# Wider weight conversions, one reciprocal per visit, and a plan that knows the PSUM banks, in a sparse attention and feed-forward kernel

## The chip, the core and the metric

The kernel runs on one core of one Trainium2 chip. The metric is the device time of one execution in microseconds (us). Three runs of the kernel before took 1224.89, 1225.10 and 1226.91 us; the median is 1225.1 us.

## What is computed

q, k and v hold 8 batches of 8 heads with 576 rows of 64 values. For each head, scores are q times k transposed, divided by 8; scores more than tau below the largest of their row are dropped; the rest go through a softmax and weight v. The heads are laid side by side to 4608 rows of 512 values, and each row x goes through a feed-forward layer.

```
scores = scale * np.matmul(q, k.transpose(0, 1, 3, 2))
thresh = np.max(scores, axis=-1, keepdims=True) - tau
scores = np.where(scores >= thresh, scores, -1000000000.0)
attn = softmax(scores); attn_out = np.matmul(attn, v)      # cut
h = x @ w_in;  r = np.maximum(h, 0.0);  g = s * (r * r) + b
out = g @ w_out
```

The weights w_in and w_out (512 x 2048 and 2048 x 512) arrive as 64-bit floats and are turned into 32-bit ones on the core.

## The kernel before, in words

**Attention.** A *visit* is one pair of heads of one batch over one half of the rows: 64 visits of four *tiles* each (two heads, two blocks of 128 rows), and in every second visit a fifth tile with the last 64 rows of both heads (288 tiles). TensorE (PE) writes a tile's 128 x 576 scores into a PSUM tile. VectorE (DVE) takes the row limit (L416, in place) and adds tau (L421); ScalarE (ACT) takes the exponential into an SBUF tile em or tr (L427); DVE reads the scores again to drop what is below the limit and sums the rest (L430), then takes the reciprocal (L433). From visit 4 on GpSimd (POOL) scales the tile by it (L435); in visits 0 to 3 (*unscaled*) the shares are put in later (L498, L520, L521). In the first 8 visits PE transposes each tile: a small block of 64 columns (L445) and four blocks of 128 (L447), which ACT copies out (L454 and L456). Later visits transpose on DVE and by DMA. After a visit's last tile PE multiplies with v (L507) into the bank pv.

**PSUM.** Five tiles hold the eight banks: s0, s1 and o have two each, pv and h one each. In visits 0 to 3 scores go round s0, s1 and o; the small transposes go back into the score tile that was just read (its first columns), the large ones into h or pv.

**Feed-forward.** After four visits a block of 256 rows is split into a high and a low part (L621 on ACT, L623 on DVE, two halves), and 16 steps f follow: 12 matmuls into h (L637), square of the positive part on ACT (L644, L645), high part (L647), low part on POOL (L648), and 6 matmuls into o (L654), three per half of the rows. L674 takes o out. 18 blocks make 288 steps.

**Weights.** For each f, 512 KB of w_in and 512 KB of w_out are loaded (L546, L549). Each half is converted by itself: ACT L582, DVE L585 (a shift) and L587 (shift and or), ACT L591, POOL L593; DVE L596 adds w_out up. The first 16 steps need one conversion each.

**The order.** Every operation is recorded with its engine, costs and the keys that it reads and writes. `Plan.run` (L62 to L88) lists them in 144 ways (18 settings by 8 rounds), plays each through a model of the engines, and keeps the best; the engines then run exactly that order. The plan before knows keys, not banks: an operation that has to wait because another engine is in the same bank is not seen by it, while the recording layer adds that wait.

Of the kernel before, what the change touches and what calls it, by code (L numbers as in the profile page):

```python
# [29 lines left out]
SCALED_LATE = 4  # L30


class Plan:
# [6 lines left out]
    SLOW = (1, 1.2), (2, 1.3), (3, 1.5), (4, 1.3)  # L40
# [6 lines left out]
    def add(self, engine, cost, emit, r=(), w=(), at=0.0, port=False, tiled=False):  # L47
# [12 lines left out]
        self.ops.append((engine, cost[0], cost[-1], emit, deps, at, port or engine == "POOL", tiled))  # L60

    def run(self):  # L62
# [7 lines left out]
        for share, later, stretch in [(a, b, c) for a in self.SHARES for b in self.LATER for c in self.STRETCH]:  # L70
            rank, early = [o[5] for o in ops], set()
            for _ in range(ROUNDS):
# [6 lines left out]
                if best is None or worth < best[0]:  # L79
                    best = worth, order  # L80
# [6 lines left out]
        self.order = best[1]  # L87
        return [ops[n][3] for _, n in self.order]  # L88

# [3 lines left out]
    def played(self, order, seed, cold, hand=60, to_pe=150, same=40):  # L93
        ops, free, done, port, mode = self.ops, {}, [0.0] * len(self.ops), 0.0, False
        late = random.Random(seed)
        for _, n in order:
            e, busy, ready, _, deps, _, shared, tiled = ops[n]
# [4 lines left out]
            for d in deps:  # L102
                if ops[d][0] != e:
                    t = max(t, done[d] + (to_pe if e == "PE" else hand))
                elif e != "PE":
                    t = max(t, done[d] + same)
            if shared and port > t:
                t = port
# [10 lines left out]
            done[n] = t + busy + tail  # L119
        return max(done) / 1000  # L120

    def ordered(self, before, after, rank, busy, done, back):
# [10 lines left out]
        order, port, mode = [], 0.0, False  # L133
        for _ in ops:
# [17 lines left out]
            if e == "PE" and mode and not ops[n][7]:  # L152
                for at, m in sorted(there[e]):
                    if ops[m][7] and at < rank[n] + self.NEAR:
# [4 lines left out]
                        break  # L159
            if e == "PE":  # L160
                t += self.TURN * (mode != ops[n][7])
                mode = ops[n][7]
            if ops[n][6] and port > t + self.PASS:
                for at, m in sorted(there[e]):
                    if not ops[m][6] and busy[m] < port - t + self.OVER:
                        there[e].remove((at, m))
                        heapq.heapify(there[e])
                        heapq.heappush(there[e], (rank[n], n))
                        n = m
                        break  # L170
            if ops[n][6]:
                t = max(t, port)
                port = t + busy[n]
            order.append((t, n))
# [17 lines left out]
def tile_attention_ffn(ctx: ExitStack, tc: tile.TileContext, qT, kT, v, tau, w_in, w_out, s, b, out):  # L192
    nc = tc.nc
    P = 128
# [29 lines left out]
    st = [const(f"st{i}", [P, 8]) for i in range(12)]  # L224
# [59 lines left out]
    class Visit:  # L284
# [10 lines left out]
        def scores_in(self, i, j):  # L295
            return f"s{i % 2}" if self.split else f"s{j}" if self.late else ("s0", "s1", "o")[i % 3]
# [59 lines left out]
    def scores(vs, i, t):  # L356
        n = vs.n
        if t is None:
# [4 lines left out]
            pe(970, both, [("k", n)] + vs.kd, ["s0"], i - SCORES_AHEAD)  # L363
# [13 lines left out]
    def split_scores(vs, i, j, t):  # L377
# [8 lines left out]
        pe(531, products, [(x, j) for x in ("z", "qh", "ql")], [sk], i - SCORES_AHEAD)  # L386
# [22 lines left out]
    def tile_of(vs, i, j, t):  # L409
        sk = vs.scores_in(i, j)  # L410
        ps, ks_, st8 = flat[sk], f"st{i % 12}", st[i % 12]
# [6 lines left out]
            scalar1=nsc, scalar2=None, op0=ALU.mult, op1=ALU.min, accum_out=st8[:, 0:1]),  # L418
            [sk, "nsc"], [sk, (ks_, 0)], i - 0.6)
        if vs.pe:  # L420
            dve((127, 208), lambda: nc.vector.tensor_scalar(  # L421
                out=st8[:, 1:2], in0=st8[:, 0:1], scalar1=tau8, scalar2=None, op0=ALU.add),
                [(ks_, 0), "nsc"], [(ks_, 1)], i - 0.4)
        else:
            act((186, 285), lambda: nc.scalar.activation(out=st8[:, 1:2], in_=st8[:, 0:1], func=AF.Identity, bias=tau8),  # L425
                [(ks_, 0), "nsc"], [(ks_, 1)], i - 0.4)
        act((632, 740), lambda: nc.scalar.activation(  # L427
            out=ev, in_=ps[:, S0:S0 + S], func=AF.Exp, bias=st8[:, 0:1], scale=-1.0),
            [sk, (ks_, 0)], [em_k], i - 0.5)
        dve((742, 830), lambda: nc.vector.scalar_tensor_tensor(  # L430
            out=eb, in0=ps[:, S0:S0 + S + 1], scalar=st8[:, 1:2], in1=eb, op0=ALU.is_le, op1=ALU.mult,
            accum_out=st8[:, 2:3]), [sk, em_k, (ks_, 1)], [em_k, (ks_, 2)], i)
        dve((90, 165), lambda: nc.vector.reciprocal(out=st8[:, 4:5], in_=st8[:, 2:3]), [(ks_, 2)], [(ks_, 4)], i)  # L433
        if not vs.unscaled:
            pool((795, 825), lambda: nc.gpsimd.tensor_scalar(  # L435
                out=ev, in0=ev, scalar1=st8[:, 4:5], scalar2=zero, op0=ALU.mult, op1=ALU.add), [em_k, (ks_, 4)], [em_k], i)

        if vs.pe:
            tt, kt = ps[0:T, 0:P], (sk, "t")
            kp = ["pv"] if vs.late or i % 2 else ["h0", "h1"]  # L440
            tp = bank[kp[0].strip("01")]
            tp = tp.rearrange("p (c q) -> p c q", c=NQ)

            def transposes():
                nc.tensor.transpose(out=tt, in_=ev[:, M:S], identity=ident)  # L445
                for c in range(NQ):
                    nc.tensor.transpose(out=tp[:, c], in_=ev[:, c * P:(c + 1) * P], identity=ident)  # L447
            pe(575, transposes, [em_k, "ident"], [kt] + kp, i + 0.5)
            parts = [(j, 4 * t, 0, P)] if t is not None else [(h, NB // 32, h * T, h * T + T) for h in range(2)]
            for h, n0, c0, c1 in parts:  # L450
                nn = (c1 - c0) // 32
                e = er[:, vs.n, h, n0:n0 + nn].rearrange("p n (c q) -> p c n q", c=5)
                ke = [("er", vs.n, h, n0 + n) for n in range(nn)]
                act((46 + 28 * nn, 146 + 28 * nn), lambda e=e, c0=c0, c1=c1, nn=nn: nc.scalar.copy(  # L454
                    out=e[0:T, NQ], in_=tt[:, c0:c1].rearrange("p (n q) -> p n q", n=nn)), [kt], ke, i + 0.5)
                act((68 + 100 * nn, 176 + 100 * nn), lambda e=e, c0=c0, c1=c1, nn=nn: nc.scalar.copy(  # L456
                    out=e[:, 0:NQ], in_=tp[:, :, c0:c1].rearrange("p c (n q) -> p c n q", n=nn)), kp + ke, ke, i + 0.5)
# [407 lines left out]
```

## Time and profile before

| | |
|---|---|
| median of three runs | 1225.1 us |
| the profiled execution | 1225.36 us, its span 1223.5 us |
| PE busy | 1194.7 us (98%) |
| DVE, ACT, POOL busy | 802.5, 766.9, 700.8 us |
| mean granted TensorE clock | 0.993 |

Busy time is the share in which an engine had something in flight. The rows below were read from the views of this execution: waits (who waited for whom, total, times, longest), windows (busy time of each engine in a stretch of the span), groups of like instructions, and the timeline (start, duration, engine, line, tile; in brackets the idle time ahead of it and what ended it). One instruction's duration is longer than the distance to the next on the same engine; where a price of an instruction in a stream is meant, it is that distance.

### The profile page before, as it was taken

To read this page: it belongs to the slowest core of one execution; us is meant where nothing else is said; L and a number is where in the kernel's file an instruction comes from. 1 tells how busy PE (TensorE), PEld (TensorE's weight loads), DVE (VectorE), ACT (ScalarE), POOL (GpSimd) and SP (SyncE) were. 2 spreads that over 40 slices of the span, in tenths; PEclk is the share of its full clock that TensorE was granted. 3 is DMA by queue.
4 is the path that set the end of the run, shared out by engine and by line. 5 is a ranking of instruction groups with operands and counts; after the bars stand their busy time and mean duration, and the time that the engine had idled before them with its cause. 6 is when DMAs were issued, how large, how long until landed. Compare 5 with 4: busy or idle time off the path is not lost.

```text
span 1223.5 us, 24575 instructions
## 1 busy us (share of the span) xinstructions
PE 1194.7 (98%) x7958; PEld 987.4 (81%) x7958; DVE 802.5 (66%) x2162; ACT 766.9 (63%) x1890; POOL 700.8 (57%) x806
## 2 busy tenths in 40 slices
PE   7789999999999999999999999999999999999998
PEld 5467778888887888878887888888888888878987
DVE  7997876777776776756666667666666576663021
ACT  5777756666665765666666666566656665654443
POOL 1466845766665775656675666667656675652200
PEclk8999999999999999999999999999999999999999
DMA  8661256677767766666566756556756666652000
GB/s 301 210 206 43 64 137 157 155 184 184 179 153 173 185 169 162 155 157 169 138 172 166 172 142 157 142 151 159 193 137 158 156 159 152 170 134 69 4 18 18
DMA packets 259536, 180.69 MB, mean 148 GB/s; under 512 B 83536, under 2 KB 238160, under 8 KB 259408
## 3 DMA queue, kind: packets, MB, share of 16 engines
q1 hardware_dynamic: 259120, 178.98, 57.5%
q8 instruction: 64, 1.05, 0.4%
q14 instruction: 64, 0.52, 0.1%
q10 hardware_dynamic: 288, 0.13, 0.0%
HBM read 87.03 MB, written 9.44 MB: 79 GB/s over the span
## 4 chain that ended last, share of the span: by engine, by line
PE 94%; DVE 3%; ACT 1%; issue 1%; DMA 0%; ACTq 0%; DVEq 0%
PE h L637 34%; PE o L654 33%; PE pv L507 13%; PE s L384 9%; PE s L373 2%; PE s L395 1%; DVE s L416 1%; DVE k L587 1%; PE pv L447 1%; DVE tr L430 0%; DMA qr<-in_q_dram 0%; DVE em L430 0%; PE s L445 0%; ACT em L427 0%; ACT er L456 0%
## 5 line engine op out<-in xcount | busy, mean ns | idle before, releaser
L637 PE MATMUL h<-xh,w 128*128 128x256 f32 x2304 | 467.0, 284 | 1.2 <-ACT g L644 1.2
L637 PEld LDWEIGHTS h<-xh,w 128*128 128x128 f32 x2304 | 377.5, 190 | 28.1 <-issue 7.6
L654 PE MATMUL o<-w,gh 128*128 128x512 f32 x1152 | 364.9, 398 | 0.6 <-DVE em L674 0.6
L416 DVE TENSOR_SCALAR_CACHE_REDUCE s<-s,nsc 128x576 f32<-128x576 f32 x283 | 230.4, 820 | 153.8 <-PE s L384 119.5
L648 POOL TENSOR_TENSOR gl<-g,gh 128x256 fp32r<-128x256 f32 x272 | 204.6, 753 | 212.7 <-ACT gh L647 187.1
L637 PE MATMUL h<-xl,w 128*128 128x256 f32 x1152 | 325.1, 282 | 0.0
L435 POOL TENSOR_SCALAR em<-em,st,zero 128x576 f32<-128x576 f32 x262 | 220.0, 841 | 139.2 <-DVE st L433 94.1
L430 DVE SCALAR_TENSOR_TENSOR em<-s,st,em 128x577 f32<-128x577 f32 x268 | 217.0, 811 | 83.9 <-ACT st L425 54.1
L427 ACT ACTIVATE em<-s,st 128x576 f32<-128x576 f32 x268 | 197.7, 738 | 66.9 <-DVE s L416 41.0
L654 PEld LDWEIGHTS o<-w,gh 128*128 128x128 f32 x1152 | 196.5, 189 | 35.1 <-issue 11.3
L654 PE MATMUL o<-w,gl 128*128 128x512 f32 x576 | 224.5, 390 | 0.0
L644 ACT ACTIVATE g<-h 128x256 f32<-128x256 f32 x288 | 110.4, 383 | 181.2 <-PE h L637 165.4
L637 PEld LDWEIGHTS h<-xl,w 128*128 128x128 f32 x1152 | 219.0, 190 | 5.5
L468 DVE STREAM_TRANSPOSE tr<-em 128x512 f32<-128x512 f32 x252 | 178.1, 707 | 52.0 <-POOL em L435 45.4
L507 PE MATMUL pv<-er,vb 128*64 128x256 f32 (+1 forms) x1280 | 170.3, 411 | 0.0
L349 POOL TENSOR_TENSOR k<-kr,k 64x576 fp32r<-64x576 f32 x104 | 149.0, 1434 | 37.1 <-ACT k L348 26.9
L647 ACT CAST gh<-g 128x256 fp32r<-128x256 f32 x288 | 116.2, 404 | 43.2 <-PE o L654 40.2
L384 PE MATMUL s<-k 128*128 128x288 f32 x832 | 142.4, 296 | 0.0
L507 PEld LDWEIGHTS pv<-er,vb 128*64 128x64 f32 x1280 | 85.7, 136 | 66.8 <-issue 11.8
L384 PEld LDWEIGHTS s<-k 128*128 128x128 f32 x832 | 127.2, 188 | 15.3 <-issue 2.4
L654 PEld LDWEIGHTS o<-w,gl 128*128 128x128 f32 x576 | 108.2, 188 | 24.6
L645 ACT ACTIVATE g<-g 128x256 f32<-128x256 f32 x288 | 120.0, 417 | 4.8
(108 smaller groups left out, 939.5 us busy)
## 6 DMA issues: line engine op xcount, KB each, us to landing
er<-tr SPq DMA_DIRECT2D x448, 160.0 KB, 3.2
kr<-in_k_dram SPq DMA_DIRECT2D x116, 288.0 KB, 4.1
vb<-in_v_dram SPq DMA_DIRECT2D x128, 128.0 KB, 3.0
qr<-in_q_dram SPq DMA_DIRECT2D x56, 160.0 KB, 4.3
er<-tr SPq DMA_DIRECT2D x112, 80.0 KB, 2.3
w<-in_moe_w_in_dram SPq DMA_DIRECT2D x16, 512.0 KB, 6.3
w<-in_moe_w_out_dram SPq DMA_DIRECT2D x16, 512.0 KB, 5.4
out_dram<-oo SPq DMA_DIRECT2D x30, 256.0 KB, 2.3
```

Source lines behind the costliest of these rows:

```text
L349: pool((1500, 1500), lambda: nc.gpsimd.tensor_tensor(out=z()[D:P], in0=kr[D:P, j], in1=z()[D:P].bitcast(F32), op=ALU.subtract), rk + [("z" ...
L384: nc.tensor.matmul(flat[sk][:, S0 + hf * HS:S0 + (hf + 1) * HS], lazy["q"][:, x, j, qc], lazy["k"][:, j, cs], start=(x == 0), stop=(x == 1))
L416: dve((740, 875), lambda: nc.vector.tensor_scalar(out=ps[:, S0:S0 + S], in0=ps[:, S0:S0 + S], scalar1=nsc, scalar2=None, op0=ALU.mult, op1 ...
L427: act((632, 740), lambda: nc.scalar.activation(out=ev, in_=ps[:, S0:S0 + S], func=AF.Exp, bias=st8[:, 0:1], scale=-1.0), [sk, (ks_, 0)], [ ...
L430: dve((742, 830), lambda: nc.vector.scalar_tensor_tensor(out=eb, in0=ps[:, S0:S0 + S + 1], scalar=st8[:, 1:2], in1=eb, op0=ALU.is_le, op1= ...
L435: pool((795, 825), lambda: nc.gpsimd.tensor_scalar(out=ev, in0=ev, scalar1=st8[:, 4:5], scalar2=zero, op0=ALU.mult, op1=ALU.add), [em_k, ( ...
L468: nc.vector.transpose(out=to[:, :, 0:NQ].rearrange("p m c q -> p m (c q)"), in_=ev[:, 0:M].rearrange("p (m r) -> p m r", m=4))
L507: nc.tensor.matmul(ps[j * D:(j + 1) * D, 0:32 * nb], vb[r, n, j, c], er[r, n, j, 0:nb, 32 * c:32 * c + 32], start=(c == 0), stop=(c == 4))
L637: nc.tensor.matmul(ps, w[:, c, :], x[:, c, :], start=(c == 0 and i == 0), stop=(c == NC - 1 and i == 2))
L645: act((322, 417), lambda: nc.scalar.activation(out=g, in_=g, func=AF.Square), [f"g{k}"], [f"g{k}"], at)
L648: do((712, 740), lambda: eng.tensor_tensor(out=lo, in0=g, in1=hi.bitcast(F32), op=ALU.subtract), [f"g{k}", f"gh{n}"], [f"gl{n}"], at)
L654: nc.tensor.matmul(bank["o"][:, t, :], a[:, ts_], w, start=(f == 0 and i == 0), stop=(f == NF - 1 and i == 2))
```

## The change

1. **Conversions 1024 wide.** Both halves of a weight step are converted together: one L655 on ACT for two L582, one L658 and one L660 on DVE for two L585 and two L587, one L663 for two L591. The two POOL operations stay. The wide operations wait until both halves have landed.
2. **One reciprocal for an unscaled visit.** Its four row sums stand side by side, and L490 runs once, after the fourth tile (4 for 16).
3. **Banks.** Unscaled visits use s0 and s1 alone for scores. Transposes leave the score tiles: in visits 0 to 3 they go to o, pv and h, from visit 4 on both kinds go to pv, the small one (L511) after the large one (L508) was copied out.
4. **The plan.** It keeps the last use of each bank and waits for it in listing and playing (`banks`, `free_at`, `used`), the prices of a few PE operations and the slow-down factors of the model are other numbers, and 28 numbers name random shifts of ranks (`shifted`) that are laid over the best order, after which the order is listed again.

```diff
+SHIFTS = (75, 80, 103, 117, 141, 184, 274, 284, 571, 923, 1025, 1061, 1146, 1562, 1708, 1768, 1775, 1850, 1896, 2348, 2463, 2483, 2540, 2693, 2702, 2859, 3035, 3099)
-    SLOW = (1, 1.2), (2, 1.3), (3, 1.5), (4, 1.3)
+    SLOW = (1, 1.0), (2, 1.1), (3, 1.3), (4, 1.1)
+    def free_at(self, n, t, last, tail, hand):
+        for b, writes in self.ops[n][8]:
+            for e, wrote, at, rest in last.get(b, ()):
+                if e != self.ops[n][0] and (writes or wrote):
+                    t = max(t, at + (rest if tail is None else tail) + hand)
+        return t
+        for n in SHIFTS:
+            rank = self.shifted(n, order, rank)
+            order = self.ordered(before, after, rank, busy, done, False)
-    st = [const(f"st{i}", [P, 8]) for i in range(12)]
+    st = [const(f"st{i}", [P, 4, 5]) for i in range(6)]
-            return f"s{i % 2}" if self.split else f"s{j}" if self.late else ("s0", "s1", "o")[i % 3]
+            return f"s{i % 2}" if self.split else f"s{j}"
-        dve((90, 165), lambda: nc.vector.reciprocal(out=st8[:, 4:5], in_=st8[:, 2:3]), [(ks_, 2)], [(ks_, 4)], i)
+        if not vs.unscaled or k_ == 3:
+            k0 = 0 if vs.unscaled else k_
+            dve((90, 165), lambda: nc.vector.reciprocal(out=sv[:, 3, k0:k_ + 1], in_=sv[:, 2, k0:k_ + 1]),
...
-            tt, kt = ps[0:T, 0:P], (sk, "t")
-            kp = ["pv"] if vs.late or i % 2 else ["h0", "h1"]
+            if vs.late:
+                tp, kp = bank["pv"], ["pv"]
+                tt, kt = tp[0:T, 0:P], kp
+            elif i % 2:
+                tt, kt, tp, kp = bank["pv"][0:T, 0:P], ["pv"], bank["o"][:, 0], ["o0"]
+            else:
+                tt, kt, tp, kp = bank["o"][0:T, 1, 0:P], ["o1"], bank["h"], ["h0", "h1"]
...
-        for u, k in (0, "i"), (1, "o"):
-            act((565, 680), lambda u=u: nc.scalar.activation(
-            dve2((340, 420), lambda u=u: nc.vector.tensor_scalar(
-            dve2((602, 686), lambda u=u: nc.vector.scalar_tensor_tensor(
+        act((1100, 1210), lambda: nc.scalar.activation(
+        dve2((607, 690), lambda: nc.vector.tensor_scalar(
+        dve2((1140, 1220), lambda: nc.vector.scalar_tensor_tensor(
...
```

The DVE at the start, before: the first two pairs of tiles (s_104 and s_105 are s0 and s1), with narrow conversions between them.

```order
L416 TENSOR_SCALAR s_104,st_71<-s_104,nsc 128x576
L416 TENSOR_SCALAR s_105,st_72<-s_105,nsc 128x576
L421 TENSOR_SCALAR st_71<-st_71,tau_67 128x1
L421 TENSOR_SCALAR st_72<-st_72,tau_67 128x1
L430 SCALAR_TENSOR_TENSOR em_83,st_71<-s_104,st_71,em_83 128x577
L585 TENSOR_SCALAR xh<-xh 128x512
L433 RECIPROCAL st_71<-st_71 128x1
L430 SCALAR_TENSOR_TENSOR em_84,st_72<-s_105,st_72,em_84 128x577
L587 SCALAR_TENSOR_TENSOR xh<-w_128,xh 128x512
L433 RECIPROCAL st_72<-st_72 128x1
L416 TENSOR_SCALAR o,st_73<-o,nsc 128x576
L416 TENSOR_SCALAR s_104,st_74<-s_104,nsc 128x576
```

The same place now (s_98 and s_99 are s0 and s1):

```order
L471 TENSOR_SCALAR s_98,st_71<-s_98,nsc 128x576
L471 TENSOR_SCALAR s_99,st_71<-s_99,nsc 128x576
L479 TENSOR_SCALAR st_71<-st_71,tau_67 128x1 x2
L485 SCALAR_TENSOR_TENSOR em_77,st_71<-s_98,st_71,em_77 128x577
L485 SCALAR_TENSOR_TENSOR em_78,st_71<-s_99,st_71,em_78 128x577
L471 TENSOR_SCALAR s_98,st_71<-s_98,nsc 128x576
L471 TENSOR_SCALAR s_99,st_71<-s_99,nsc 128x576
L479 TENSOR_SCALAR st_71<-st_71,tau_67 128x1 x2
```

The second pair now uses the tiles that the first one has just left, and no conversion stands between them. Later pairs have wide conversions between them, as here between the pairs of visit 2 (DVE now):

```order
L485 SCALAR_TENSOR_TENSOR em_78,st_73<-s_99,st_73,em_78 128x577
L660 SCALAR_TENSOR_TENSOR k<-w_195,k 128x1024
L595 TENSOR_TENSOR x_85<-pv,x_85 128x256
L668 TENSOR_TENSOR bias_t<-bias_t,k 128x512
L658 TENSOR_SCALAR k<-k 128x1024
L471 TENSOR_SCALAR s_98,st_73<-s_98,nsc 128x576
```

Every pair from the third on has one to five such operations between its end and the next pair's scores. PE at the first feed-forward step, before (tile 16 and 17 are em_83 and em_84):

```order
L362 MATMUL s_104<-kr,k 128x288 x2
L445 MATMUL s_104<-k,em_83 64x128
L447 MATMUL pv<-k,em_83 128x128 x4
L445 MATMUL s_105<-k,em_84 64x128
L447 MATMUL pv<-k,em_84 128x128 x4
L637 MATMUL h<-xh,w_280 128x256
L637 MATMUL h<-xl,w_280 128x256
```

And now (em_77, em_78 and tr_79 are tiles 16 to 18):

```order
L508 MATMUL pv<-k,em_77 128x128 x4
L511 MATMUL pv<-k,em_77 64x128
L709 MATMUL h<-xh,w_252 128x256
L709 MATMUL h<-xl,w_252 128x256
L709 MATMUL h<-xh,w_252 128x256 x2
L709 MATMUL h<-xl,w_252 128x256
L709 MATMUL h<-xh,w_252 128x256
L415 MATMUL s_98<-kr,k 128x288 x2
L508 MATMUL pv<-k,em_78 128x128 x4
L511 MATMUL pv<-k,em_78 64x128
L508 MATMUL pv<-k,tr_79 128x128 x4
L709 MATMUL h<-xh,w_252 128x256
```

The first half of the step (six matmuls) now stands ahead of the fifth tile's scores and of tile 17's transposes, the second half behind tile 18's.

## Rows read from the trace of the kernel before

**Rows 1.** The page: busy time (share, instructions) and 40 slices of the span.
```profile
PE 1194.7 (98%) x7958; PEld 987.4 (81%) x7958; DVE 802.5 (66%) x2162; ACT 766.9 (63%) x1890; POOL 700.8 (57%) x806
PE   7789999999999999999999999999999999999998
```
**Rows 2.** Windows: start:end length, busy (instructions) of each engine, PEclk, DMA.
```profile
10.00:40.00 30.00, 23.29 (x141) 14.62 (x141) 28.51 (x81) 22.52 (x47) 7.96 (x6) 0.87 0.83 286
40.00:70.00 30.00, 21.65 (x131) 13.30 (x131) 28.51 (x80) 20.70 (x43) 12.33 (x10) 0.89 0.66 211
78.00:150.00 72.00, 69.96 (x463) 52.63 (x463) 58.89 (x142) 55.48 (x141) 51.95 (x52) 1.00 0.22 67
150.00:1130.00 980.00, 980.00 (x6608) 818.48 (x6607) 665.19 (x1808) 621.71 (x1550) 609.45 (x705) 1.00 0.64 158
```
**Rows 3.** Waits of PE, 72 to 150 us.
```profile
PE s L445 <- ACT tr L427: 1.5, 1, 1.5
PE s L445 <- DVE tr L430: 1.3, 1, 1.3
PE pv L447 <- ACT er L456: 0.6, 1, 0.6
PE h L637 <- ACT g L644: 0.2, 1, 0.2
```
**Rows 4.** Timeline of DVE from its first tile on.
```profile
8.57 0.82 DVE L416 TENSOR_SCALAR_CACHE_REDUCE s<-s,nsc 128x576 f32<-128x576 f32 x1 [2.66 <-PE s L373]
9.32 0.82 DVE L416 TENSOR_SCALAR_CACHE_REDUCE s<-s,nsc 128x576 f32<-128x576 f32 x1
10.06 0.39 DVE L421 TENSOR_SCALAR st<-st,tau 128x1 f32<-128x1 f32 x2
10.41 0.82 DVE L430 SCALAR_TENSOR_TENSOR em<-s,st,em 128x577 f32<-128x577 f32 x1
11.15 0.42 DVE L585 TENSOR_SCALAR xh<-xh 128x512 int32<-128x512 int32 x1
11.49 0.16 DVE L433 RECIPROCAL st<-st 128x1 f32<-128x1 f32 x1
12.29 0.69 DVE L587 SCALAR_TENSOR_TENSOR xh<-w,xh 128x512 int32<-128x512 int32 x1
12.89 0.15 DVE L433 RECIPROCAL st<-st 128x1 f32<-128x1 f32 x1
```
**Rows 5.** Timeline of DVE and PE around the first staging and the first step.
```profile
69.47 0.68 DVE L623 TENSOR_TENSOR xl<-x,xh 128x512 fp32r<-128x512 f32 x1
70.84 0.36 PE L637 MATMUL h<-xh,w 128*128 128x256 f32 x1
72.23 0.28 PE L637 MATMUL h<-xh,w 128*128 128x256 f32 x1
```
**Rows 6.** Groups of DVE by shape, 8.5 to 69.5 us: busy, mean ns.
```profile
L587 DVE SCALAR_TENSOR_TENSOR k<-w,k 128x512 int32<-128x512 int32 x11 | 10.0, 906 | 0.0
L585 DVE TENSOR_SCALAR k<-k 128x512 int32<-128x512 int32 x12 | 5.7, 483 | 0.0
```
**Rows 7.** Timeline of PE: scores of a pair, at either clock.
```profile
60.66 1.97 PE L373 MATMUL s<-kr,qr 64*128 64x288 f32 x8
72.44 1.24 PE L373 MATMUL s<-kr,qr 64*128 64x288 f32 x8
```
**Rows 8.** Timeline of PE: from L654 into L507, and into L654.
```profile
83.01 0.39 PE L654 MATMUL o<-w,gl 128*128 128x512 f32 x1
83.33 3.06 PE L507 MATMUL pv<-er,vb 128*64 128x320 f32 x20
90.37 0.39 PE L654 MATMUL o<-w,gl 128*128 128x512 f32 x1
90.60 0.62 PE L654 MATMUL o<-w,gh 128*128 128x512 f32 x2
```
**Rows 9.** Timeline of DVE and PE at the end of the span.
```profile
1214.58 0.43 DVE L648 TENSOR_TENSOR gl<-g,gh 128x256 fp32r<-128x256 f32 x1 [2.40 <-ACT gh L647]
1218.25 0.74 PE L654 MATMUL o<-w,gh 128*128 128x512 f32 x2 [0.58 <-DVE em L674]
1219.26 1.27 DVE L674 SCALAR_TENSOR_TENSOR em<-o,s_t,bias_t 128x256 f32<-128x256 f32 x3 [1.07 <-PE o L654]
```

More of the change, by code (lines that the diff above doesn't have):

```diff
@@ L94, in played @@
         ops, free, done, port, mode = self.ops, {}, [0.0] * len(self.ops), 0.0, False
-        late = random.Random(seed)
+        late, last = random.Random(seed), {}
         for _, n in order:
-            e, busy, ready, _, deps, _, shared, tiled = ops[n]
+            e, busy, ready, _, deps, _, shared, tiled, _ = ops[n]
             t = free.get(e, 0.0)
@@ L106, in played @@
                     t = max(t, done[d] + same)
+            if ops[n][8]:
+                t = self.free_at(n, t, last, None, to_pe if e == "PE" else hand)
             if shared and port > t:
@@ L119, in played @@
             done[n] = t + busy + tail
+            if ops[n][8]:
+                self.used(n, t + busy, tail, last)
         return max(done) / 1000
@@ L132, in ordered, with delay @@
                 heapq.heappush(coming[o[0]], (0.0, n))
-        order, port, mode = [], 0.0, False
+        order, port, mode, last = [], 0.0, False, {}
+        def delay(n, t):
+            at = max(t, port) if ops[n][6] else t
+            if not ops[n][8]:
+                return at - t
+            hand = self.TO_PE if ops[n][0] == "PE" else self.HANDOVER
+            return self.free_at(n, at, last, done[n] - busy[n] if back else None, hand) - t
         for _ in ops:
@@ L159, in ordered @@
                         break
+            wait = delay(n, t)
+            if wait > self.PASS:
+                for at, m in sorted(there[e]):
+                    if delay(m, t) <= self.PASS and busy[m] < wait + self.OVER:
+                        there[e].remove((at, m))
+                        heapq.heapify(there[e])
+                        heapq.heappush(there[e], (rank[n], n))
+                        n, wait = m, delay(m, t)
+                        break
+            t += wait
             if e == "PE":
@@ L162, in ordered @@
                 mode = ops[n][7]
[L163 to L170, printed above, removed]
             if ops[n][6]:
-                t = max(t, port)
                 port = t + busy[n]
+            if ops[n][8]:
+                self.used(n, t + busy[n], done[n] - busy[n], last)
             order.append((t, n))
@@ L410, in tile_of @@
         sk = vs.scores_in(i, j)
-        ps, ks_, st8 = flat[sk], f"st{i % 12}", st[i % 12]
+        k_ = i - vs.first if vs.pe else 0
+        ps, ks_, sv = flat[sk], f"st{(vs.order if vs.pe else i) % 6}", st[(vs.order if vs.pe else i) % 6]
+        low, limit, total, share = (sv[:, x, k_:k_ + 1] for x in range(4))
         m = i % 4 if vs.pe else i % 2
@@ L458, in tile_of @@
+            pe(390, whole, [em_k, "ident"], kp, i + 0.5)
+            if kt != kp:
+                pe(90, rest, [em_k, "ident"], kt, i + 0.5)
+            copies(True)
+            if kt == kp:
+                pe(90, rest, [em_k, "ident"], kt, i + 0.5)
+            copies(False)
             return
@@ L508, in products @@
                                      start=(c == 0), stop=(c == 4))
-        more = [(f"st{(vs.first + k) % 12}", 4) for k in range(4)] + ["ident"] if vs.unscaled else []
+        more = [(f"st{vs.order % 6}", 4, k) for k in range(4)] + ["ident"] if vs.unscaled else []
         return (170 + 267 * nb + 450 * vs.unscaled, products, more +
@@ L726, in guards @@
     def guards():
[L727 removed]
+        for n in "s0", "s1":
             nc.vector.memset(flat[n][:, S0 + S:S0 + S + 1], -3e38)
```

116 lines of the change are left out of this document (71 added, 45 removed).

## The prediction, as it was put on record

> **What bounds the kernel now.** I read the page first: PE is busy 98% of the span, and in the 40 slices only the first three and the last fall short [rows 1]. Then the windows by stage. From 150 to 1130 us PE is busy all the time (980.00 of 980), so there a faster DVE, ACT or POOL buys nothing, and only PE's own work can shrink. From 10 to 70 us it is the other way round: DVE is busy 28.51 of 30 us, twice, and PE 23.29 and 21.65 [rows 2]. DVE sets when the first block is staged, and what comes behind is PE's. Then the waits of PE after its first step: four, 3.6 us in all, three of them about a transpose or its copy [rows 3]. So three stretches can move: DVE's way to the first staging, PE's few waits up to 150 us, and the last microseconds.
>
> **Prices on DVE.** From start to start [rows 4]: limit 0.74, both small adds 0.35 (0.13 each in a stream), masking 0.74, narrow shift 0.34, narrow or 0.60, reciprocal 0.08. Staging and the weight sum I take as 0.61, close to the or, which also reads two tensors of 512; the product of L521, 256 wide, as 0.35. The wide operations are not in the trace. A wide shift lies between 0.34 (width free) and 0.68 (two narrow ones), a wide or between 0.60 and 1.20. One staging of 512 columns takes 0.68 and one L648 on DVE of 256 takes 0.43 [rows 5, 9]: about 1 ns a column. So an or of 1024 costs 0.60 + 0.53 = 1.13; the shift, at 0.34 for 512, can have a slope of about half that, and I take 0.61. Both are near the upper ends, as the slope is.
>
> **DVE's way to the first staging.** Before, its order has ahead of the first L623: 21 limits, 20 adds, 20 maskings, 16 shifts, 18 reciprocals, 15 ors, 6 sums and 4 products: 15.5 + 2.6 + 14.8 + 5.4 + 1.5 + 9.0 + 3.7 + 1.4 = 53.9. From 8.57 to 69.47 it took 60.9 [rows 4, 5], 7.0 more. Of that, idle time is about 3.0 (the two windows leave 1.49 each [rows 2]). The other 4.0 is in stretched conversions: 11 ors at 906 ns instead of 0.69 (2.4 us), 12 shifts at 483 instead of 0.42 (0.8 us) [rows 4, 6], rounding in the rest. They stretch while POOL works.
>
> Now there stand ahead of it 20 limits, 20 adds, 18 maskings, 9 wide shifts, 8 wide ors, 8 sums, 6 reciprocals (two of them for a whole visit) and 4 products: 14.8 + 2.6 + 13.3 + 5.5 + 9.0 + 4.9 + 0.5 + 1.4 = 52.0, which is 1.9 less.
>
> *Stretch.* POOL's work is the same, but DVE starts half as many conversions that can run into it. Bounds: nothing saved, or all 4.0. I take 1.4, as a start that meets POOL is now rarer but waits as long.
> The Trainium skill speaks against more (SBUF — State Buffer, Who interferes with whom): VectorE and GpSimd share one pair of ports, the first holds it for a whole instruction, and the other is blocked. A wide instruction would hold it twice as long. By that rule alone nothing is saved here, and the total below is 1.4 us worse. The stretched rows agree that someone is blocked; no row shows a wide one.
>
> *Idle.* With two score tiles a pair can only be scored when the pair before has been masked. A pair's scores take 1.24 us, or 1.97 at the low clock [rows 7]; with hand-offs DVE is bare about 1.5 us if nothing stands between. At the first two turns nothing does: 2 x 1.5. The next seven turns have operations of 2.4 to 4.0 us between them (2.7 in the piece shown: 1.13 + 0.35 + 0.61 + 0.61), enough for the scores and for the transposes that PE does ahead of them; about 1 us in all at the two where the copies of o come late, and 1.5 for the rest of the way. That makes 5.5 us idle for 3.0, 2.5 more. Bounds: none more, or nine turns at 1.5, less the 3.0 of before, which is 10.5 more.
>
> First staging: 69.47 − 1.9 − 1.4 + 2.5 = 68.7. The second half comes later than before: two maskings, two reciprocals, one limit and the half itself (1.5 + 0.2 + 0.7 + 0.6), and that limit waits about 0.6 for scores that PE does behind the first six matmuls. The second six start at about 68.7 + 3.6 + 0.6 + 0.2 = 73.1 and end at 73.8, against 72.35 before (the last of the twelve starts at 72.23 [rows 5]). By then PE has transposed one tile more, 0.6 of work. Net: **0.85 us lost**.
>
> **PE after its first step.** The waits of 1.5 and 1.3 us are small transposes into a score tile whose neighbour in the bank is being read, that of 0.6 is pv not yet copied [rows 3]. The score tiles no longer take transposes. In their place PE's order has two spots where a tile's small transpose stands right behind its large one, and two where the next large one follows a small one, all in pv; elsewhere 6 or 12 matmuls of the feed-forward layer stand between. The two right behind each other before the second six are hidden under the staging. I take 1.0 for the rest (bounds 0 and 4 x 0.8): **2.5 us won**. By tile 26 PE's order has about 4 us more feed-forward work ahead of the transposes than before, so a late tile stops it less easily.
>
> **Mode changes.** Going from L654 into L507 takes 0.32 from start to start, where L654 to L654 takes 0.23 [rows 8]: 0.09 for the change to matmuls on half the rows or columns. The way back I take as the same. Counted in PE's order there are 188 before and 176 now; in the stretch where PE is full (from the second block on) 134 and 120. 14 x 0.09 = **1.3 us won**. Bounds 0.6 (the way back free) and 1.9.
>
> **The end.** The last three matmuls before waited 0.58 for DVE's first take, although it reads the other half of o [rows 9]; in PE's order now no such wait stands there. Then four takes follow instead of three, 0.42 each: **0.3 won** (bounds 0 and 0.7).
> The Trainium skill (PSUM — Partial Sum Buffer, PSUM bank collisions raise a hardware error) has engines kept apart by bank. The two halves of o are two banks, so by it that wait need not be, nor, early in the changed kernel, that of a transpose into one half of o for a copy from the other; the idle term would be 1 us smaller. The row shows that waits here go by the tile.
>
> **Elsewhere nothing.** ACT is busy 22.52 and 20.70 of 30 us early [rows 2], and one wide operation for two narrow ones adds nothing to it. The SP queue issues the weights about as early as before. If a w_out lands late, the wide conversion waits for it with its whole step; the two to four steps converted ahead are the cover.
>
> **Sum.** 1225.36 + 0.85 − 2.5 − 1.3 − 0.3 = 1222.1 for an execution like the profiled one, which is 0.26 over the median; so 1221.9.
>
> **Rivals.**
> *More is won.* All nine later turns are covered, the stretch falls by 3, and the plan's knowledge of banks leaves PE without waits up to 150 us: staging at 65.6, 3.1 earlier, and 1.0 more on PE: 1217.8. For it: DVE has cover at almost every turn. Against: two bare turns at the start are certain.
> *Nothing arrives.* The staging is late by as much as PE's waits give back, through pv: per tile a large and a small transpose and two copies there in turn, and values in between. Then the 2.5 us of PE's waits are missing: 1221.9 + 2.5 = 1224.4. For it: one bank where there were three.
> *Slower: two score tiles starve DVE.* If a turn is bare about 1.5 us at all nine instead of two and a bit, DVE idles 8 us more than I count: 1221.9 + 8 = 1229.9. It decides where the wide conversions between two pairs are not ready, as they need both loads and stand in ACT's queue between exponentials, and DVE executes in order. It turns slower than before at 3 us more, two or three turns. Against: early on the DMA engines are busy 0.83 of the time and ACT three quarters [rows 2], so both have room.
>
> **Chances.** Forecast 0.40 (1220 to 1224), more 0.25, nothing 0.22, slower 0.13. About 0.2%, 2.5 us, is what a measurement of this kernel can tell from no change, so faster means below 1222.6: 0.70 of the forecast and all of "more" give 0.53, with a little of "nothing" 0.55; slower 0.11; the rest 0.34. The range takes "more" in almost whole and reaches to a lost turn on the other side: 1217 to 1226.5.
>
> **What would show it.** In the profile after: the first staging at 68 to 70 us; wide shifts of about 0.7 and wide ors of about 1.2 us in their rows, some longer; DVE waiting for scores for 1 to 2 us twice before 20 us, hardly later; PE's waits between 74 and 150 us below 1.5 us; no wait of L726 for DVE at the end. I am wrong if DVE waits for scores in most turns (slower), if PE's first step comes before 67 us (more), or if PE waits in pv again and again up to 125 us (nothing).

## The result: 0.6% slower

The changed kernel takes 1234.38 us (median of five runs), the kernel before in the same comparison 1225.87 us: ratio 1.0058, 95% interval 1.0046 to 1.0069. The forecast was 1221.9 us, with a range of 1217 to 1226.5. The direction is that of the fourth case, two score tiles that starve VectorE, and the size is more than that case gave. The profiled execution took 1233.11 us with a span of 1231.3 us, 7.8 us more than the 1223.5 before.

The page after, against [rows 1]: DVE has less to do, PE is busy longer, and the first two slices stand at 6 tenths where they stood at 7.

```profile
PE 1197.4 (97%) x7958; PEld 989.2 (80%) x7958; DVE 792.0 (64%) x2117; ACT 762.3 (62%) x1858; POOL 701.4 (57%) x806
PE   6689999999999999999999999999999999999998
```

The windows after, against [rows 2] (columns as there). From 10 to 40 us DVE is busy 22.58 us instead of 28.51, and the granted clock, as a share of 2.4 GHz, is 0.67 instead of 0.87. From 150 us on PE, full before, has 3.7 us without work.

```profile
10.00:40.00 30.00, 23.07 (x128) 13.81 (x128) 22.58 (x54) 18.34 (x33) 8.17 (x6) 0.67 0.76 255
150.00:1130.00 980.00, 976.34 (x6587) 812.92 (x6587) 665.65 (x1818) 616.67 (x1553) 609.37 (x706) 1.00 0.69 158
```

The timeline of DVE from its first tile on, against [rows 4]. After the first two tiles (one limit stands here) nothing is left to do, twice. The bracket is the idle time and what ended it.

```profile
7.82 0.83 DVE L471 TENSOR_SCALAR_CACHE_REDUCE s<-s,nsc 128x576 f32<-128x576 f32 x1 [2.06 <-PE s L426]
...
14.13 0.82 DVE L471 TENSOR_SCALAR_CACHE_REDUCE s<-s,nsc 128x576 f32<-128x576 f32 x1 [2.90 <-PE s L426]
...
21.03 0.83 DVE L471 TENSOR_SCALAR_CACHE_REDUCE s<-s,nsc 128x576 f32<-128x576 f32 x1 [2.65 <-PE s L426]
```

The timeline of PE in the same stretch. It waits for the masks (L485), then scores the next pair, while DVE waits. The pair at 11.81 takes 2.29 us, that at 29.73 takes 1.24 ([rows 7] had 1.97 and 1.24); the value products take 4.62 us here. The granted clock is 0.50 from 10 to 28 us: the lower of its two levels, 1.2 GHz.

```profile
10.63 0.39 PE L511 MATMUL o<-k,em 128*64 128x128 f32 x1 [2.82 <-DVE em L485]
11.81 2.29 PE L426 MATMUL s<-kr,qr 64*128 64x288 f32 x8
...
25.18 4.62 PE L581 MATMUL pv<-er,vb 128*64 128x256 f32 x20
29.73 1.24 PE L426 MATMUL s<-kr,qr 64*128 64x288 f32 x8
```

In the kernel before the third score tile let PE go on at this place: it scored into o while DVE was at the first pair.

```profile
8.33 1.16 PE L373 MATMUL o<-kr,qr 64*128 64x288 f32 x2
```

The first staging, before and after. Its halves started at 69.47 [rows 5] and 70.27 us, and start at 72.31 and 76.67 now.

```profile
70.27 0.67 DVE L623 TENSOR_TENSOR xl<-x,xh 128x512 fp32r<-128x512 f32 x1
```
```profile
72.31 0.68 DVE L695 TENSOR_TENSOR xl<-x,xh 128x512 fp32r<-128x512 f32 x1
76.67 0.69 DVE L695 TENSOR_TENSOR xl<-x,xh 128x512 fp32r<-128x512 f32 x1
```

The first step's twelve products into h follow. The last of them started at 72.23 us [rows 5] and starts at 79.35 now. Two transposes in the value bank stand between the second half of the staging and the second six products, and wait:

```profile
77.42 0.30 PE L511 MATMUL pv<-k,em 128*64 128x128 f32 x1 [0.68 <-ACT er L520]
78.29 0.63 PE L508 MATMUL pv<-k,tr 128*128 128x128 f32 x4 [0.57 <-ACT er L523]
...
79.35 0.28 PE L709 MATMUL h<-xh,w 128*128 128x256 f32 x1
```

The groups of DVE by shape, against [rows 6] (busy us, mean ns): the wide operations have the price that was forecast.

```profile
L660 DVE SCALAR_TENSOR_TENSOR k<-w,k 128x1024 int32<-128x1024 int32 x6 | 7.3, 1222 | 0.0
L658 DVE TENSOR_SCALAR k<-k 128x1024 int32<-128x1024 int32 x7 | 5.1, 734 | 0.0
```

The waits of PE (us in total, times, longest), against [rows 3]: first 78 to 150 us (without one of 0.2), then 150 to 1130, where there was none before. The first and the last line of the second are block ends, where a first product into h waits for the staging, and products into o for a take of one of its halves.

```profile
PE pv L508 <- ACT er L523: 2.2, 2, 1.6
PE pv L581 <- ACT er L523: 0.4, 1, 0.4
```
```profile
PE h L709 <- DVE xl L695: 1.3, 1, 1.3
PE h L709 <- ACT g L716: 1.2, 3, 0.5
PE o L726 <- DVE oo L746: 1.1, 4, 0.3
```

The end, against [rows 9]: PE's wait of 0.58 is gone, and four takes follow its last product.

```profile
1226.58 1.66 DVE L746 SCALAR_TENSOR_TENSOR em<-o,s_t,bias_t 128x256 f32<-128x256 f32 x4 [3.06 <-PE o L726]
```

**Where the 7.8 us are.** Nearly all of them are lost by the end of the first step. The first 318 matmuls, the twelve products among them, were issued by 73.02 us before and are by 79.58 now (the two orders differ in four of them, scores for transposes; one in flight at the cut counts on both sides). Of these 6.6 us, 3.9 are idle time of PE (19.5 and 23.3 us) and 2.7 are the length of the matmuls (53.56 and 56.27 us busy). Behind them PE is busy the same 1141.1 us, and its idle time up to the end of the span is 10.6 us instead of 9.4.

```profile
0.00:73.02 73.02, 53.56 (x318) 0.88 0.75 248
73.02:1224.00 1150.98, 1141.09 (x7642) 1.00 0.57 141
```
```profile
0.00:79.58 79.58, 56.27 (x318) 0.79 0.74 235
79.58:1232.00 1152.42, 1141.11 (x7641) 1.00 0.61 141
```

### The profile page after: what moved, and what is told of

It is laid out like the page before. It is cut to its first block, busy times and chain, and to the rows that moved or that the text cites. A ratio compares the mean times of both kernels' runs of the same rounds, so it can differ in the third digit from the quotient of the medians.

```text
span 1231.3 us, 24436 instructions
## 1 busy us (share of the span) xinstructions
PE 1197.4 (97%) x7958; PEld 989.2 (80%) x7958; DVE 792.0 (64%) x2117; ACT 762.3 (62%) x1858; POOL 701.4 (57%) x806
## 4 chain that ended last, share of the span: by engine, by line
PE 93%; DVE 2%; DMA 2%; ACT 1%; issue 1%; SPq 0%; POOL 0%; DVEq 0%; ACTq 0%; POOLq 0%
PE h L709 33%; PE o L726 32%; PE pv L581 13%; PE s L437 9%; PE s L426 2%; PE s L448 1%; DMA qr<-in_q_dram 1%; DVE s L471 1%; PE pv L508 1%; DMA w<-in_moe_w_out_dram 0%; ACT em L482 0%; PE s L415 0%; DVE em L485 0%; ACT tr L482 0%; PE o L508 0%
## 5 line engine op out<-in xcount | busy, mean ns | idle before, releaser
L726 PE MATMUL o<-w,gh 128*128 128x512 f32 x1152 | 365.9, 399 | 1.1 <-DVE oo L746 1.1
L471 DVE TENSOR_SCALAR_CACHE_REDUCE s<-s,nsc 128x576 f32<-128x576 f32 x288 | 233.5, 821 | 148.1 <-PE s L437 105.2
L485 DVE SCALAR_TENSOR_TENSOR em<-s,st,em 128x577 f32<-128x577 f32 x270 | 218.7, 813 | 108.3 <-ACT st L476 66.9
L726 PEld LDWEIGHTS o<-w,gh 128*128 128x128 f32 x1152 | 196.0, 189 | 35.8 <-issue 9.8
L726 PE MATMUL o<-w,gl 128*128 128x512 f32 x576 | 224.6, 390 | 0.0
L581 PE MATMUL pv<-er,vb 128*64 128x256 f32 (+1 forms) x1280 | 172.8, 415 | 0.4 <-ACT er L523 0.4
L726 PEld LDWEIGHTS o<-w,gl 128*128 128x128 f32 x576 | 108.2, 188 | 24.6
```

Of the source, the lines that this page charges most:

```text
L471: dve((740, 875), lambda: nc.vector.tensor_scalar(out=ps[:, S0:S0 + S], in0=ps[:, S0:S0 + S], scalar1=nsc, scalar2=None, op0=ALU.mult, op1 ...
L485: dve((742, 830), lambda: nc.vector.scalar_tensor_tensor(out=eb, in0=ps[:, S0:S0 + S + 1], scalar=limit, in1=eb, op0=ALU.is_le, op1=ALU.mu ...
L581: nc.tensor.matmul(ps[j * D:(j + 1) * D, 0:32 * nb], vb[r, n, j, c], er[r, n, j, 0:nb, 32 * c:32 * c + 32], start=(c == 0), stop=(c == 4))
L726: nc.tensor.matmul(bank["o"][:, t, :], a[:, ts_], w, start=(f == 0 and i == 0), stop=(f == NF - 1 and i == 2))
```

## Experiments

Theory A: with two score tiles the first four visits go in bare turns, DVE waits for PE and PE for DVE, and PE's clock falls as it waits, which makes the turns longer. Rivals: B, the wide conversions come too late to fill the turns; C, the new plan's order and its shifts are bad; D, the transposes now queue in the value bank. Times are medians of 4 to 12 runs. Where the order is "the changed kernel's own", nothing moves on any engine; "planned anew" means that the order is another too, so that a microsecond or two of a single comparison may be its luck.

**Keeping PE busy (changed kernel, its own order).** `fill(k, bank)` issues k products of ones and zeros of 256 columns.
```
 first pair of scores:      + fill(10, "pv")
 transposes of tiles 1, 3:  + fill(8, "h")
 last of the 16 at start:   + fill(6, "h")
```


> The changed kernel in its own order on every engine; only TensorE gets 32 more products whose results nobody reads: 6 behind the sixteen at the start, 10 behind the first pair of scores, 8 behind the transposes of the second tile and 8 behind those of the fourth, where the trace of the changed kernel shows TensorE idle (1.55, 2.82, 2.18 and 2.08 us). Theory A (in the bare first turns TensorE stands idle, its clock therefore stays at the low level up to 25.7 us, and scores, transposes and value products at twice their length make the turns longer still): the clock rises by about 14 us instead of 25.7, the second pair of scores takes near 1.3 us instead of 2.29, the value products 2.5 instead of 4.62, the first staging ends 3 to 4 us earlier than 72.3, and the run takes 1229 to 1231. Rival (the clock is not what costs; the turns are bare whatever the clock): the products fill idle time, the staging ends within 0.5 us of 72.3, the run stays at 1233 to 1235.


Measured: 1228.54 us, ratio 1.0016 [1.0007, 1.0025]; 5.8 us of the 8.5 are back, more than forecast. The granted clock is 1.00 from 10 to 14 us, 0.50 in the changed kernel, where it rises between 28 and 30 us and not at 25.7 as expected above. The timeline of PE shows the pair and the value products of above at their short lengths, and that of DVE the two halves of the staging at 67.73 and 72.34:

```profile
11.72 1.24 PE L430 MATMUL s<-kr,qr 64*128 64x288 f32 x8
...
21.02 2.48 PE L589 MATMUL pv<-er,vb 128*64 128x256 f32 x20
```
```profile
67.73 0.68 DVE L703 TENSOR_TENSOR xl<-x,xh 128x512 fp32r<-128x512 f32 x1
72.34 0.69 DVE L703 TENSOR_TENSOR xl<-x,xh 128x512 fp32r<-128x512 f32 x1
```
What came back is length, not waiting. 26 of the products take 3.8 us in PE's timeline (ten of them the 1.46 below, the eights at 13.38 and 18.20 1.19 each), so of its 1196.8 busy microseconds at most 1193.0 are the kernel's own, 4.4 less than in the changed kernel.

```profile
8.18 1.46 PE L411 MATMUL pv<-gh,oo 128*128 128x256 f32 x10
```
The time in which PE does no work of the kernel's own (idle, or at these products) is at least 34.1 us here, 33.9 in the changed kernel and 28.8 before. So the waits stay. The filling takes away length, and more of it than the 2.7 us that the change had added, since the kernel before has low stretches too.

The first half of the staging now begins 1.7 us earlier than before the change ([rows 5]), 1.0 earlier than forecast, and the kernel is still 2.5 us slower. Its second half, though, is 2.1 us later than the 70.27 of before, and the last of the first twelve products 2.8 us later than the 72.23: the time of the run goes with the end of the first step, not with the start of the staging.

```profile
74.99 0.28 PE L717 MATMUL h<-xh,w 128*128 128x256 f32 x1
```

**The same on the kernel before (its own order).**
```
 first pair of scores:     + fill(10, "pv")
 last of the 16 at start:  + fill(6, "h")
```


> The kernel before, in its own order on every engine, with 16 products more whose results nobody reads: 6 behind the sixteen at the start and 10 behind the first pair of scores. Theory A (the changed kernel alone fell into a long low clock, the kernel before had 10 us of it at the start): it gains too, but less than the 5.9 us of the changed kernel: 1223 to 1225 (the scores and transposes between 6.9 and 13.7 us ran at half speed, about 2 us). Rival (warm products shorten any kernel of this program by the same 5 to 6 us, and the changed kernel's loss is not the clock): 1220 to 1221.


Measured: 1227.32 us, 1.0006 [0.9998, 1.0015]: nothing, against both expectations. The low clock only came later. Four large transposes, 1.06 us at 13.72 and 0.60 at 18.82 in the kernel before, are short first and long then in PE's timeline:

```profile
12.06 0.60 PE L453 MATMUL h<-k,em 128*128 128x128 f32 x4
...
17.36 1.06 PE L453 MATMUL pv<-k,tr 128*128 128x128 f32 x4
```

**Transposes: late ones (changed kernel, its own order).**
```
-  tt, kt = tp[0:T, 0:P], kp      # visits 4 to 7: value bank
+  tt, kt = ps[0:T, 0:P], kp      # the tile's own score tile
```


> The changed kernel in its own order on every engine; only the small transposes of visits 4 to 7 (20 instructions) and their copies go through the score tile again, as before the change, instead of through the value bank. Theory D (the second half of the first staging and the steps behind it are late because in that bank large transposes, copy, small transposes and copy follow one another): the wait of 1.43 us of the small transposes at 72.7 us is gone, the second half of the staging ends 1 to 2 us earlier against the first (4.36 us apart now), the run takes 1232 to 1233. Theory A alone: these waits are beside others, the run stays within 0.5 us of 1234.4.


Measured: 1235.52 us, 1.0075 [1.0060, 1.0090]. No gain. PE's wait of 1.43 us for a copy at 72.7 is gone, and at nearly the same place it waits for a mask:

```profile
71.80 0.42 PE L511 MATMUL s<-k,em 128*64 128x128 f32 x1 [2.28 <-DVE tr L485]
```

**Transposes: early ones (changed kernel, its own order, with the 32 products).**
```
-  tt = bank["pv"][0:T, 0:P]         # odd tiles, visits 0 to 3
+  tt = bank["o"][0:T, 1, P:2 * P]
```


> The changed kernel in its own order with the 32 products of the first experiment, and the small transposes of the odd tiles of visits 0 to 3 go to the second half of the o bank instead of the value bank (no instruction more or less, none moved). Theory D1 (the rest of the loss, 2.5 us, are the waits of these transposes for VectorE's product that reads the value bank, 3.11 us at 28.9 and 1.36 us at 53.3): both waits go, 1225 to 1227. Rival (TensorE waits there for the next instruction instead, since VectorE is what is late): the waits come back under another name, 1228 to 1229.


Measured: 1229.44 us, 1.0018 [1.0009, 1.0028], as the first experiment without it (1.0016). The waits for L603 at 28.9 and 53.3 us are gone from PE's timeline. The one below stands near the first, and another of 1.79 us for a mask 2 us behind it; near the second, a wait of 3.09 us at 56.65 has become 4.67. D falls with both.

```profile
27.23 0.42 PE L519 MATMUL o<-k,em 128*64 128x128 f32 x1 [2.97 <-ACT er L531]
```

**Parts of the change, planned anew.** The edits take whole functions of one kernel into the other; the core of each:
```
 wide alone (e3):       kernel before + wide conversions
 two tiles (e8):        kernel before + scores_in -> f"s{j}" + new transposes
 wide, two tiles (e12): both
 no shifts (e7):        changed kernel, SHIFTS = ()
 three tiles (e4):      changed kernel, scores_in -> ("s0", "s1", "o")[i % 3],
                        transposes of before, the 28 shifts kept
 three, no shifts (e11): the same with SHIFTS = ()
```


> The changed kernel with the planner, the three score tiles and the transposes of the kernel before, and a reciprocal for each tile: what is left of the change is the conversions 1024 columns wide (planned anew). Theory A (two score tiles make the turns bare, the wide conversions are only too late to fill them): with three score tiles DVE finds other work, TensorE keeps its clock, 1222 to 1227. Rival B (the wide conversions, ready at 19 us instead of 10, take the fill away in any plan): DVE has waits of 2 to 3 us for scores before 22 us here too, clock low up to 25 us, 1230 to 1235.


Measured: 1227.36 us, 1.0005 [0.9997, 1.0014]. With three tiles the wide conversions cost and win nothing. B falls: the timeline of DVE has, after the first, no longer wait for scores before 29 us than this.

```profile
12.13 0.83 DVE L418 TENSOR_SCALAR_CACHE_REDUCE o<-o,nsc 128x576 f32<-128x576 f32 x1 [0.70 <-PE o L373]
```

> The kernel before with one part of the change: the first four visits use two score tiles and the transposes go to the o, value and h banks in the new way; conversions 512 columns wide, a reciprocal for each tile, the old planner without shifts (planned anew). Theory A (two score tiles alone are enough): waits of over 2 us for scores at the start, a low clock beyond 20 us, 1230 to 1236. Rival B (the narrow conversions, ready at 10 us, fill the turns): no such wait, 1224 to 1228.


Measured: 1233.50 us, 1.0061 [1.0039, 1.0082]: all of the loss, with narrow conversions and the old planner. That is the time that theory A named, but not by bare turns of DVE. Conversions fill the turns of DVE: up to 70 us it waits 5.2 us for scores, 3.3 of them for the first, where the changed kernel waits 9.4, 2.1 of them for the first. It is PE that waits here, 11.6 us in five waits for masks; in the changed kernel five such waits take 10.1, in the kernel before all of them 7.4. PE is busy 1195.0 us, as before the change (1194.7), so here the loss is waiting, and not longer matmuls. Of the 7.4 us by which the span is longer, 4.1 stand ahead of the last 7640 matmuls and 3.3 behind. The waits of DVE for scores, of the eighth experiment and of the changed kernel (us in total, times, longest):

```profile
DVE s L418 <- PE s L373: 5.2, 5, 3.3
```
```profile
DVE s L471 <- PE s L426: 9.4, 6, 2.9
```
The waits of PE for masks, of the eighth experiment, the changed kernel and the kernel before:

```profile
PE h L455 <- DVE tr L432: 8.8, 4, 4.2
PE h L455 <- DVE em L432: 2.8, 1, 2.8
```
```profile
PE o L511 <- DVE tr L485: 5.4, 2, 3.2
PE o L511 <- DVE em L485: 2.8, 1, 2.8
PE h L508 <- DVE tr L485: 1.1, 1, 1.1
PE h L508 <- DVE em L485: 0.8, 1, 0.8
```
```profile
PE s L373 <- DVE tr L430: 2.9, 2, 2.4
PE s L373 <- DVE em L430: 1.8, 1, 1.8
PE o L445 <- DVE tr L430: 1.6, 1, 1.6
PE s L362 <- DVE tr L430: 0.9, 1, 0.9
PE s L445 <- DVE tr L430: 0.2, 1, 0.2
```

> The changed kernel's conversions, reciprocal, two score tiles and transposes in the old planner, without shifts: against the eighth experiment (1233.5) only the conversions' width and the reciprocal differ, against the seventh (1240.95) only the planner. Theory A with B as its helper (two tiles make bare turns, wide conversions, ready at 19 us instead of 10, leave them unfilled): 1236 to 1242, slower than the eighth by 3 us or more. If the width doesn't matter for that: 1231 to 1235.


Measured: 1234.57 us, 1.0070 [1.0058, 1.0082], 1.1 us above the eighth. The width hardly matters here either.

> The changed kernel without its 28 shifts of ranks (an empty list, so that the planner's own best order stands); tiles, banks, conversions and planner stay. Theory A: the first turns are bare in this order too (two score tiles, no conversion ready before 19 us), 1231 to 1237. Rival C (the shifts, chosen for times that the chip doesn't have, made the order bad): DVE's waits of 2.9 and 2.65 us are gone, 1225 to 1229.


Measured: 1240.95 us, 1.0116 [1.0100, 1.0132]. That is above both expectations. C falls as it was put: the shifts are worth 6.6 us to the changed kernel. The bank-aware planner costs 6.4 us against the twelfth, so they give back about as much; that it is the same time is not shown.

> The changed kernel with the three score tiles of the first four visits and the transposes of the kernel before; the wide conversions, the one reciprocal and the new planner with its 28 shifts stay (planned anew, so that a difference below some 2 us is also that of another order). Theory A: the waits of 2.9 and 2.65 us for scores go below 1 us, the clock is high by about 14 us, the run takes 1225 to 1229. Rivals: B (the wide conversions are the cause) and C (the new planner's order is): 1231 to 1236, with the first staging ending after 71 us.


Measured: 1232.32 us, 1.0047 [1.0030, 1.0064]: 2 us better than the changed kernel, and where rivals B and C put it, with the first staging at 74.55 us. But the shifts had been chosen for another order, so this run tells little; the next is the clean one.

> The changed kernel without its 28 shifts, as the seventh experiment, and with the three score tiles and the transposes of the kernel before, as the fourth, whose shifts were chosen for another order. Against the seventh (1240.95), only tiles and transposes differ, both in the new planner's own order. Theory A: three tiles are worth 6 us or more here too, 1229 to 1235. Rival (the bank-aware planner makes bad orders whatever the tiles): 1238 to 1243.


Measured: 1231.31 us, 1.0047 [1.0030, 1.0065], 9.6 us below the seventh, in the new planner.

**The number of tiles alone.** Two tiles with the transposes of the kernel before, first with nothing else of the change that counts, then in the changed kernel without shifts. In both, as in every kernel here with two tiles, the plan also books the taking out of one half of o under that half alone.
```
-  ("s0", "s1", "o")[i % 3]
+  f"s{j}"
```


> The kernel before with two score tiles instead of three in the first four visits and nothing else of the change that counts: 512 columns wide, a reciprocal for each tile, the old planner without shifts (planned anew), and the transposes as before, the small ones into the tile's own score tile, the large ones into h and the value bank. The eighth experiment (1233.5) had two tiles and the new transposes. If the third tile is what is missing: 1231 to 1237, DVE waits for scores at the start. If the split of the transposes and their new banks cost: 1225 to 1229.


Measured: 1236.19 us, 1.0082 [1.0070, 1.0095].


> The seventh experiment (wide conversions, one reciprocal, the bank-aware planner without shifts, two score tiles: 1240.95) with the transposes of the kernel before. Against the eleventh (1231.3) only the number of score tiles differs. If the third tile is what is missing: 1238 to 1243 as the seventh. If the new transposes cost: 1229 to 1234 as the eleventh.


Measured: 1241.65 us, 1.0128 [1.0113, 1.0144].
In both plans the third tile is worth about 10 us (1226.3 to 1236.2; 1231.3 to 1241.7), and the new transposes do no harm (1236.2 to 1233.5, 1241.7 to 1241.0). The time is lost at the start: the last 7640 matmuls begin at 73.03 and 84.85 us in the first pair, at 75.40 and 86.79 in the second. In the first pair PE is busy 1194.7 and 1202.5 us, so 7.8 of the 12.0 us by which the span is longer are length. Up to 70 us PE waits 14.1 us for masks and limits of DVE in the first of the two experiments:

```profile
PE s L450 <- DVE tr L432: 5.8, 2, 3.4
PE s L450 <- DVE em L432: 4.4, 2, 2.8
PE s L450 <- DVE s L418: 3.9, 2, 2.2
```

One chain of runs leads from one kernel to the other, each step one part (the first with the booking of o and a few prices of the plan): 1226.3, two tiles 1236.2, new transposes 1233.5, wide conversions and one reciprocal 1234.6, bank-aware planner 1241.0, shifts 1234.4.

**Shifts for the three-tile plans.** 24 and 43 seeds in the old planner, chosen by the planner's own estimate of the order.
```
 wide (e9):    SHIFTS = (169, 186, 223, ..., 3306, 3502)
 narrow (e10): SHIFTS = (5, 41, 54, ..., 3360, 3502)
```


> The third experiment's kernel (wide conversions; three score tiles, transposes and planner of the kernel before) with 24 shifts of ranks of its own, chosen for that plan as the changed kernel's 28 were for its own. The shifts were worth 6.5 us to the changed kernel (1240.95 without them, 1234.38 with). Theory (the shifts and the wide conversions are sound, the two score tiles are what costs): 3 to 6 us below the third experiment's 1227.4, so 1221 to 1224, faster than both kernels. Rival (the shifts only repair a bad order and have nothing to win where three tiles give TensorE work): 1226 to 1228.


Measured: 1226.35 us, 0.9999 [0.9990, 1.0008].


> The kernel before (512 columns wide, a reciprocal for each tile, three score tiles, the old planner, the shares kept in the changed kernel's layout) with 43 shifts of ranks chosen for its own plan. If the shifts alone bring a gain: 1220 to 1224, level with the experiment beside it, and the wide conversions are worth nothing by themselves; if the wide conversions count (4 DVE microseconds less in the first 70 us), it is 1 to 3 us slower than that one.


Measured: 1224.57 us, 0.9989 [0.9980, 0.9998]: the fastest of all, 1.4 us below the kernel before, so faster than both, though within the 0.2% called no change. So shifts won 6.6 us on the order of the seventh experiment and 1.0 and 1.4 on these two; the wide conversions win nothing here either.

## Why the prediction was wrong

**The step that failed is the idle term of "DVE's way to the first staging"**: "DVE is bare about 1.5 us if nothing stands between. At the first two turns nothing does: 2 x 1.5." That there are two bare turns was right; three things in the term were not. From its first tile to the first staging DVE took 64.5 us for 60.1 forecast: 9.0 us idle for 5.5, and 55.5 at work for 54.6. The staging began at 72.31 us instead of 68.7.

*Their length.* They took 2.90 and 2.65 us. The term had scores at 1.24 or 1.97 us and a hand-off; the chain in a turn is masks, a tile's transposes of 0.39 and 1.06 us, scores of 2.29, all at the low clock (0.50). DVE's waits for scores after the first came to 7.4 us up to 70 us (2.90, 2.65, 0.80, 0.44, 0.59).

*The clock.* It was taken as given; it follows PE's waits. With the waits filled the first experiment has the high level from 10 to 14 us where the changed kernel has the low one, the same pair takes 1.24 us instead of 2.29, and 5.8 us are back. In the kernel before, 16 such products only moved the low stretch. How a loss with two tiles divides into waits and length depends on the order: 2.7 of 7.8 us are length in the changed kernel, next to nothing in the eighth experiment, 7.8 of 12.0 in the thirteenth. The Trainium skill tells of a kernel whose matmuls wait for transfers (TensorE: Matmul & The Clock Gate, HAM oscillation — how this bites in real kernels), and there each wait puts the clock back to the low level. The rows of the changed kernel agree, with waits for another engine.

*Whose time it is.* The term counted DVE's half of a turn alone. Seven of nine turns were covered by conversions, so DVE was seen busy and the turn held to be free. But with two tiles PE has to wait out the masks, covered or not: 11.6 us in the eighth experiment, one wait of 4.2, where DVE itself waits little, and 7.4 with the third tile. The kernel before had a third tile to score. So the right rival had the wrong condition: it decides not "where the wide conversions between two pairs are not ready", since two tiles cost the same with narrow ones (1233.5 and 1234.6).

**From the first half of the staging to the end of the first step** the prediction counted too little again. The second half came 4.36 us behind the first, for 3.6: it waited 1.26 us for scores, for 0.6. The second six products started 2.0 us behind that, for 0.8: the two transposes held to be hidden under the staging were not, and waited 0.68 and 0.57 us in the value bank. They started at 78.67 us, 5.6 later than the 73.1 of the prediction. That is half of the 11.0 us by which the sum missed the profiled execution (1222.1 and 1233.11), and the idle term is the largest part of it.

**The other half lies behind the first step**, in "PE after its first step", 2.5 us won, in "Mode changes", 1.3 won, and in waits that were not forecast. Up to 150 us the waits behind the first step fell from 3.6 to 2.2 us (0.21, 1.58, 0.40), so 1.4 were won. But behind 150 us, where there was none, 3.7 us came. The second experiment shows that moving the small transposes out of the value bank wins nothing: what PE waits for there is late itself. Of the mode changes nothing is to be seen: behind the first 318 matmuls PE is busy 1141.09 us before and 1141.11 now.

**What held.** The wide or at 1.22 us and the wide shift at 0.69 to 0.73; less DVE work; no wait of L726 for DVE at the end. With four takes for three, 4.8 us pass there behind PE's last product instead of 4.3, so little of the 0.3 is left. That DVE work is saved was right and worth nothing: wide conversions are at 1.0005 with three tiles.

**What stays open.** Why the bank-aware planner costs about 5 us with either number of tiles (1227.4 to 1231.3, 1234.6 to 1241.0) was not followed up, nor all of the new waits at block ends. Of their 3.7 us, 1.1 are products into o that wait for a take. Such waits from 100 to 1130 us stand in all nine kernels whose plan books a take under one half of o, and in none of the others; no run changes that alone.

## What to carry to other kernels

When a change takes a buffer from a loop in which two engines take turns, write out one turn for both: what each does while the other works. Filler on one engine hides only that engine's wait. And where a part of the program is full on one engine, follow the other engine to the date by which the full one has done the same work, not to the first sign of it: here the end of the first step told the loss, and the first half of the staging did not. A wait on TensorE before that date can also cost the clock behind it.

## What the runs showed of the hardware

Products that nobody reads gave 5.8 us in one kernel (32 of them) and nothing in the other (16, ratio 1.0006), where the low clock only moved, from transposes at 13.7 us to those at 17.4. The granted clock in the profile is not complete: in the eighth experiment its window of 0 to 20 us has 0.99, and yet the pair scored at 7.20 us takes the 2.29 us of the low level, in the timeline of PE:

```profile
0.00:20.00 20.00, 11.38 (x48) 0.99 0.87 290
```
```profile
7.20 2.29 PE L373 MATMUL s<-kr,qr 64*128 64x288 f32 x8 [2.17 <-DMA qr<-in_q_dram]
```
The Trainium skill warns of that (TensorE: Matmul & The Clock Gate, Seeing it yourself); the length of a known instruction is the surer sign.
